# Attention and FFN, forward and backward on one core: filling products split into four 32-column tiles in half of the steps, and backward stores issued from SP

## The chip, the core and the metric

The kernel runs on one core of one Trainium2 chip. The metric is the device time of one execution in microseconds (us); three runs of the kernel before gave 1441.34 us as the median, from 1441.24 to 1441.88. Five engines work beside each other, each with an instruction queue of its own that is run in order: PE (TensorE: matrix products and, as PEld, weight loads), DVE (VectorE), ACT (ScalarE), POOL (GpSimd) and SP (SyncE, which here only issues DMAs). Products land in PSUM, a small memory of banks of 128 partitions by 2 KB, and DVE or ACT have to read them out.

## The reference

The output is a block with two branches, and the gradients of all its inputs:

```
xn  = layernorm(x)                                     # x: 2048 x 448
out = x + softmax(q k^T / sqrt(28)) v wo + (silu(xn wg) * (xn wu)) wd
        with q, k, v = xn wqkv                         # 16 heads of 28
outputs: out, and d(out)/d(x, wqkv, wo, wg, wu, wd) applied to grad_out
```

All inputs and outputs are bf16. The FFN is 448 x 1792. In the attention backward, per head, P = exp(q k^T / sqrt(28)) is computed again, dP = dO v^T, dS = P * (dP - delta), dV = P^T dO, dK = dS^T q, dQ = dS k; the division by the softmax sums is folded into dO.

## The kernel before

A forward part comes first, up to about 620 us. It computes attention and FFN, transposes, and spills what the backward part needs to DRAM. It is not touched by the change. The backward part runs from about 620 to 1397 us, and a tail of some 40 us finishes the gradient of x.

**The order of the backward part is written by hand, in one loop (L1231) over steps k.** The heads are taken in 4 groups g of 4 heads, in 2 pairs hp per group. Per pair there are 4 blocks of 512 keys (kc) by 16 blocks of 128 queries (qc, qi): 512 steps in all. Four steps (qi = 0 to 3) are called a block here, 128 in all. The text names a step by m = k % 4: step 1, 2, 3, 0. Each step issues, in this order:

- `row(k)` (L804): for two heads the scores sb (L812) of step k, and dP as db (L820) of step k-1. Each is a 32-row by 128-column tile of the array with 512 moving columns; the four lie beside each other in the array.
- `ew(k)` (L832): ACT takes the exponential of both sb into e_sb (L836); DVE multiplies both db of step k-1 with it into ds_sb (L842); SP issues a DMA transpose of ds_sb into dsT (L829), in three of four steps.
- `flush(k)` (L799): the stores that have been held for two steps. `drop()` (L757): SP issues some of the loads that are due later.
- `kv(k)` (L904, two in step 1 and two in step 2 for the most part): dV and dK, four products per call, each in a 128-row by 32-column tile of the array (L915, L919), accumulated in the bank acc.
- in step 1 `dq_unit` (L936): dQ from dsT, 16 products in 32-column tiles (L946), evacuated by ACT (L959 or L950), added up by POOL (L961, L963).
- in step 0 `tr_unit` (L892): eight PE transposes of the fourth ds_sb (L897), in full 128 x 128 form, copied by ACT (L902).

**Filling products.** Between these, PE gets products of other parts, here called F: `late_dw` (L881), `y_unit` (L1072, the output), `dx_unit` (L1128) and `dc_unit` (L1172) (two parts of the gradient of x) and `dwq_unit` (L1011, the gradient of wqkv). Each is a generator that issues one product per piece, with 128 x 128 weights and 256 to 448 moving columns. `fill_open` (L1209) takes the next unit, `fill_step(room)` (L1219) issues pieces until the room in ns is used up. Step 2 issues one or two pieces (R2 = 250), right behind the two `kv` calls; step 3 four to six (R3 = 750), behind the `row`; step 0 two or three (R0 = 400) ahead of the transposes and the rest of the unit behind them. So a block holds one unit. There is one bank genb for the units and dQ together. When a unit is done, DVE or ACT reads genb.

**Buffers that set the order.** Three banks for sb, freed by the exponential three products before; three for db and the transposes together, freed by DVE's L842 (or ACT's L902); ten buffers ds_sb, freed when `kv`, the transposes and the DMA transpose have read them; three buffers dsT.

**Stores.** `store(o, i)` (L795) puts a store on a list, and `flush` issues it two steps later from POOL (L802): dkv and dqT (to DRAM, for `dc_unit` later), y, the gradients of wqkv (dwq_o) and the last slice of the FFN weight gradients. There are 76 of them, up to 128 KB each. In the tail `store` issues at once.

Of the kernel before, what the change touches and what calls it, by code (L numbers as in the profile page):

```python
# [17 lines left out]
D = 448  # L18
# [3 lines left out]
G = 4  # L22
HP = 32
NT = S // 128
NFC = F // 128
P = 128
# [77 lines left out]
def kernel(  # L104
# [23 lines left out]
    PE, DVE, ACTE, POOL, SP = nc.tensor, nc.vector, nc.scalar, nc.gpsimd, nc.sync  # L128
# [19 lines left out]
    xn_sp = xn_t[:, :NT * D].rearrange("p (t d) -> p t d", d=D)  # L148
# [399 lines left out]
    for i in range(len(chain) + LEAD):  # L548
# [4 lines left out]
        k = i - LEAD  # L553
# [100 lines left out]
    for t in range(4):  # L654
        run(T_unit(xnT, xn_t, t, t % 2 == 0, ps_s if t < 2 else None))
    DVE.tensor_reduce(out=r_ones[:],
                      in_=ident_f[:].rearrange("p (a b) -> p a b", b=HP)[:, :, 28:30],
# [11 lines left out]
    for c in range(3):  # L669
        k = 4 * c  # L670
        t = 4 * c + 4
# [100 lines left out]
    def have(*keys):  # L772
        for x in [x for x in slow if x[1] in keys]:
            slow.remove(x)
            SP.dma_start(out=x[2], in_=x[3])
# [19 lines left out]
    def store(o, i):  # L795
        held.append((now + 2, o, i))
        flush(0 if now < NB else 10 ** 9)

    def flush(upto):  # L799
        while held and held[0][0] <= upto:  # L800
            _, o, i = held.pop(0)
            POOL.dma_start(out=o, in_=i)  # L802

    def row(k):  # L804

# [51 lines left out]
    k = n = 0  # L857
# [14 lines left out]
    fT = bk.tile([P, 4, 2, 4, P], BF16, name="dsp", bufs=1)  # L872
# [3 lines left out]
    def late_dw(c):  # L876
        d0, dn = DCH[c]
        have(("f",))
        ps = ps_g.tile([P, 2, P], FP32, name="genb")
        for t in range(NT):  # L880
            PE.matmul(ps[:dn], lhsT=xn_sp[:, t, d0:d0 + dn], rhs=fT[:, t // 4, :, t % 4, :],  # L881
                      start=(t == 0), stop=(t == NT - 1))
            if t < NT - 1:
                yield 110
        DVE.tensor_copy(out=w2[:dn, c], in_=ps[:dn])
        for a, o in enumerate((out_4, out_5)):
            store(o[d0:d0 + dn, F - P:], w2[:dn, c, a])
        yield 110

    dq_acc = bk.tile([P, S // 2], FP32, name="dq_acc", bufs=1)  # L890

    def tr_unit(b):  # L892
        for qi in (3,) if b < NB // 4 - 1 else (2, 3):
# [93 lines left out]
    dsp = {}  # L987
# [19 lines left out]
    def dwq_unit(g, c, tag="genb"):  # L1007
        d0, dn = DCH[c]
        ps = (ps_b if tag == "rest" else ps_g).tile([P, 3 * P], FP32, name=tag, bufs=2 if tag == "rest" else 1)
        for t in range(NT):  # L1010
            PE.matmul(ps[:dn, :], lhsT=xn_sp[:, t, d0:d0 + dn], rhs=dsp[g][:, t].rearrange("p k r -> p (k r)"),  # L1011
                      start=(t == 0), stop=(t == NT - 1))
            if t < NT - 1:
                yield 162
        o = bk.tile([P, 3, 4, DH], BF16, name="dwq_o")
        p4 = ps[:].rearrange("p (k h r) -> p k h r", k=3, r=HP)
        cp = ACTE.copy if tag == "rest" else DVE.tensor_copy
        cp(out=o[:dn, 0], in_=p4[:dn, 0, :, :DH])
        cp(out=o[:dn, 1:3, 0:2, :], in_=p4[:dn, 1, :, :DH].rearrange("p (k h) r -> p k h r", k=2))
        cp(out=o[:dn, 2, 2:4, :], in_=p4[:dn, 2, 0:2, :DH])  # L1020
        cp(out=o[:dn, 1, 2:4, :], in_=p4[:dn, 2, 2:4, :DH])
        store(wq_out[d0:d0 + dn, :, g * 4 * DH:(g + 1) * 4 * DH],
              o[:dn].rearrange("p k h r -> p k (h r)"))
        s_done.add((g, c))
        yield 162
# [4 lines left out]
    NH = NFC // 2  # L1030
    ych, yts = {}, {}
# [16 lines left out]
    wd_sb = yp.tile([P, NFC, D], BF16, name="wd_sb", bufs=1)  # L1048
    wo_sb = yp.tile([P, G, D], BF16, name="wo_sb", bufs=1)
# [10 lines left out]
    def y_unit(ch, half, ti):  # L1060
        if ti == 0:
            have(("y", ch, half))
            nxt = 2 * ch + half + 2
            if nxt < 8:
                load_y(nxt // 2, nxt % 2)
        tsl = slice(ti * P, (ti + 1) * P)
        mm = [(ych[ch, half][:, i, tsl], wd_sb[:, half * NH + i, :]) for i in range(NH)]
        if half:
            mm += [(ych[ch, 3][:, i, tsl], wo_sb[:, i, :]) for i in range(G)]
        ps = ps_g.tile([P, 512], FP32, name="genb")  # L1070
        for i, (l, r) in enumerate(mm):
            PE.matmul(ps[:, :D], lhsT=l, rhs=r, start=(i == 0), stop=(i == len(mm) - 1))  # L1072
            if i < len(mm) - 1:
                yield 189
        if half == 0:
            yts[ti] = yp.tile([P, D], FP32, name="yt", bufs=5)
            DVE.tensor_tensor(out=yts[ti][:], in0=ps[:, :D], in1=ych[ch, 2][:, ti, :], op=ALU.add)
        else:
            y = yp.tile([P, D], BF16, name="y")
            DVE.tensor_tensor(out=y[:], in0=ps[:, :D], in1=yts[ti][:], op=ALU.add)  # L1080
            store(out0_d[:, 4 * ch + ti, :], y[:])
        yield 189


    dxs = {}
# [22 lines left out]
    def load_dx(ch, fq):  # L1108
        f0, f1 = FQ[fq]
        if ch == 2 and fq < 2:  # L1110
            load_w(fq + 1, now + 32)
        d = dxs["pool"].tile([P, 5, 2, 512], BF16, name="dau_c")
        drip(("dx", ch, fq), [(d[:, i - f0:min(i + 2, f1) - f0], F_d[ch, :, i:min(i + 2, f1), 1:3, :]) for i in range(f0, f1, 2)], now + 16)
        dxs[ch, fq] = d

    def dx_unit(ch, fq, ti):
        if ti == 0:
            have(("dx", ch, fq))
            nxt = 4 * fq + ch + 1
            if nxt < 12:  # L1120
                load_dx(nxt % 4, nxt // 4)
        d = dxs[ch, fq]
        f0, f1 = FQ[fq]
        n = 2 * (f1 - f0)
        tsl = slice(ti * P, (ti + 1) * P)
        ps = ps_g.tile([P, 512], FP32, name="genb")
        for i in range(n):
            PE.matmul(ps[:, :D], lhsT=d[:, i // 2, i % 2, tsl], rhs=dxs["w", fq][:, i // 2, i % 2, :],  # L1128
                      start=(i == 0), stop=(i == n - 1))
            if i < n - 1:  # L1130
                yield 189
        o = dxs["g"][:, 4 * ch + ti, :]
        if fq == 0:
            ACTE.copy(out=o, in_=ps[:, :D])
        else:
            DVE.tensor_tensor(out=o, in0=ps[:, :D], in1=o, op=ALU.add)
        yield 189
# [3 lines left out]
    dcs, dy2 = {}, {}  # L1141
# [23 lines left out]
    def dc_unit(t):  # L1165
        if t % 4 == 0:
            have(("dc", t // 4))
            if t < 12:
                load_dc(t // 4 + 1)
        ps = ps_g.tile([P, 512], FP32, name="genb")  # L1170
        for i in range(3 * G - 3):
            PE.matmul(ps[:, :D], lhsT=dcs[t // 4][:, i, (t % 4) * P:(t % 4 + 1) * P], rhs=dxs["wq"][:, i, :],  # L1172
                      start=(i == 0), stop=(i == 3 * G - 4))
            if i < 3 * G - 4:
                yield 189
        DVE.tensor_tensor(out=dxs["g"][:, t, :], in0=ps[:, :D], in1=dxs["g"][:, t, :], op=ALU.add)
        yield 189
# [41 lines left out]
    def fill_step(room):  # L1219
        nonlocal cur  # L1220
        if cur is None:
            return
        for ns in cur:
            room -= ns
            if room < ns / 2:
                return
        cur = None
# [3 lines left out]
    for k in range(NB + 12):  # L1231
        now = k
        if k < NB:
            g, hp, kc, qc, qi = steps[k]
            if hp == 1 and kc > 0 and qc == 2 and qi == 2 and g + 1 < G:
                load_k(g + 1, kc - 1)
            if g > 0 and hp == 0 and kc == 0 and qc == 2 and qi == 2:
                load_k(g, 3)
            if hp == 1 and g + 1 < G and qi == 3 and (kc, qc) in NEXT:
                load_q(g + 1, NEXT.index((kc, qc)))  # L1240
        m = k % 4
        if k <= NB:
            if k >= K0:
                row(k)
                ew(k)
            flush(k)
            if 2 <= k:
                drop()
        if m:
            while kv_n < NB and kv_n <= k - (2 if m == 2 or kv_n % 16 == 15 else 3) and (m != 2 or kv_n % 16):  # L1250
                kv(kv_n)
                kv_n += 1
        if m == 0:
            b = (k - 8) // 4
            if 9 <= k < NB and cur is None:
                fill_open(600)
            fill_step(R0)
            if 0 <= b < NB // 4:
                tr_unit(b)
            fill_step(BIG)  # L1260
        elif m == 1:
            b = (k - 13) // 4
            if 0 <= b < NB // 4:
                dq_unit(b)
        elif m == 2:
            if 9 <= k < NB:
                fill_open(BIG)
                fill_step(R2)
        else:
            fill_step(R3)  # L1270
    while stream:
        for _ in stream.pop(0)[1]():
            pass
# [14 lines left out]
    g = G - 1  # L1288
# [96 lines left out]
```

## Time and profile before

| | |
|---|---|
| median of 3 runs | 1441.34 us |
| the profiled execution | 1441.88 us, of which the span from the first to the last instruction is 1440.1 us |
| mean granted TensorE clock | 0.985 |
| busy: PE / ACT / DVE / POOL | 92% / 88% / 80% / 28% of the span |
| busy from 1100 to 1200 us: PE / DVE / ACT | 96.8 / 95.3 / 94.1 us of 100 |
| busy from 690 to 890 us: PE / DVE / ACT | 187.6 / 183.4 / 182.1 us of 200; DMA engines 1.16 |
| time of a block in the backward part | 5.6 to 7 us, mostly 5.63 to 6.1 |

How it is read: a line of the profile's groups gives line, engine, operation, tiles out<-in, shapes and count, then busy us and the mean ns of one, then the engine's idle time just before these instructions with what ended it. "32*128" in front of a shape is the tile of the array that a product uses (rows * columns). A timeline line gives start and length in us; equal instructions that follow each other are merged, and a wait stands in brackets. A product's record lasts some 180 ns longer than its share of the array, since products are pipelined: what counts is the distance of starts. The DMA share is the mean busy share of 16 DMA engines; it passes 1 since packets of two queues, or neighbours of one queue, overlap.

### The profile page before, as it was taken

What the parts mean: (1) busy time and instruction counts of PE and PEld (TensorE: products, weight loads), DVE (VectorE), ACT (ScalarE), POOL (GpSimd) and SP (SyncE); (2) the same over time, 40 slices, a digit from 0 to 9 for tenths busy, and PEclk for the clock granted to TensorE, in tenths of its full rate; (3) what the DMA queues carried; (4) which work ended last, traced back from release to release, by engine and by line L of the source; (5) the groups of instructions that cost most, each with busy time, mean ns of one, the idle gap of its engine ahead of it and who ended that gap; (6) DMA issues with size and microseconds to landing.
All of it is one profiled execution on the core that took longest, in us unless ns stands there. A gap on an engine that the chain in (4) does not pass through costs nothing. (4 is left out here: it accounts for less than half of the span.)

```text
span 1440.1 us, 34682 instructions
## 1 busy us (share of the span) xinstructions
PE 1326.3 (92%) x12647; PEld 541.0 (38%) x12708; DVE 1151.8 (80%) x1997; ACT 1261.5 (88%) x2193; POOL 403.6 (28%) x561
## 2 busy tenths in 40 slices
PE   5889999999999999889999999999999999999996
PEld 2333333333333333333333434433443444444343
DVE  6667757666676676578998998888889999989988
ACT  5789988988889999869989989899989999989974
POOL 6464524464334454111112112201111011010006
PEclk9999999999999999989999999999999999999998
DMA  5796956796678586799999999999999999999971
GB/s 154 181 199 165 235 122 160 187 195 164 146 162 192 147 172 145 178 234 226 226 213 217 232 220 188 196 209 229 228 173 194 209 223 230 201 191 203 198 142 60
DMA packets 681179, 271.69 MB, mean 189 GB/s; under 512 B 606424, under 2 KB 655824, under 8 KB 681008
## 3 DMA queue, kind: packets, MB, share of 16 engines
q1 hardware_dynamic: 672576, 255.35, 87.1%
q0 software_dynamic: 7024, 13.82, 4.1%
q8 instruction: 100, 1.64, 0.5%
q14 instruction: 71, 0.58, 0.1%
q10 hardware_dynamic: 1408, 0.30, 0.1%
HBM read 65.09 MB, written 60.36 MB: 87 GB/s over the span
## 5 line engine op out<-in xcount | busy, mean ns | idle before, releaser
L842 DVE TENSOR_TENSOR ds_sb<-db,e_sb 128x512 bf16<-128x512 f32 x1024 | 646.8, 684 | 51.3 <-issue 21.1
L836 ACT ACTIVATE e_sb<-sb 128x512 bf16<-128x512 f32 x1024 | 554.8, 611 | 60.4 <-PE db L820 44.5
L612 ACT ACTIVATE eT<-s_w 128x1024 bf16<-128x1024 f32 x256 | 263.5, 1029 | 46.1 <-PE s_ps L609 43.1
L614 ACT ACTIVATE eT<-s_ps 128x512 bf16<-128x512 f32 x512 | 280.4, 612 | 0.0
L820 PE MATMUL db<-kd,qd 32*128 32x512 bf16 x1024 | 234.4, 384 | 8.2 <-DVE ds_sb L842 7.4
L812 PE MATMUL sb<-kd,qd 32*128 32x512 bf16 x1024 | 210.4, 387 | 5.1 <-DMA qd<-QD_d 3.3
L961 POOL TENSOR_TENSOR dq_acc<-dq_acc,dq_st 128x256 f32<-128x256 f32 x64 | 46.2, 721 | 455.4 <-ACT dq_st L959 455.4
L919 PE MATMUL acc<-ds_sb,qd 128*32 128x512 bf16 x1024 | 161.0, 391 | 0.0
L915 PE MATMUL acc<-e_sb,qd 128*32 128x512 bf16 x1024 | 158.8, 391 | 1.3 <-DVE dw_o L528 1.3
L902 ACT COPY dsT<-db 128x1024 bf16<-128x1024 bf16 x128 | 130.1, 1016 | 14.6 <-PE db L897 13.9
L380 POOL TENSOR_TENSOR nn<-nn,ag 128x512 f32<-128x512 f32 x56 | 71.2, 1271 | 252.2 <-DVE ag L378 243.7
L609 PE MATMUL s_ps<-QQ,KK 32*128 32x512 bf16 x512 | 125.4, 385 | 3.9
L1128 PE MATMUL genb<-wguT,dau_c 128*128 128x448 bf16 x448 | 117.5, 355 | 6.3 <-ACT dq_st L959 3.9
L609 PE MATMUL s_w<-QQ,KK 32*128 32x512 bf16 x512 | 100.3, 387 | 13.1 <-ACT eT L612 10.4
L812 PEld LDWEIGHTS <-qd 32*128 32x128 bf16 x1024 | 48.2, 91 | 149.4 <-issue 140.3
L421 PE MATMUL gen<-xn_t,f_sp 128*128 128x448 bf16 x416 | 91.8, 354 | 2.6 <-DVE nn L395 1.7
L421 PEld LDWEIGHTS <-f_sp 128*128 128x128 bf16 x640 | 55.7, 98 | 75.0 <-issue 31.9
L946 PE MATMUL genb<-dsT,kd 128*32 128x256 bf16 x2048 | 79.5, 275 | 1.9 <-DVE dqT L955 0.6
L897 PE MATMUL db<-ident_bf,ds_sb 128*128 128x128 bf16 x1032 | 79.4, 220 | 1.1 <-DVE ds_sb L842 1.1
L897 PEld LDWEIGHTS <-ds_sb 128*128 128x128 bf16 x1032 | 68.3, 99 | 24.1 <-issue 5.3
L451 PE MATMUL gen<-eT,VS 128*32 128x512 bf16 x1024 | 68.4, 384 | 5.5 <-DVE nn L395 3.3
L381 POOL TENSOR_TENSOR nn<-nn,tt 128x512 f32<-128x512 f32 x56 | 72.0, 1286 | 4.4
(167 smaller groups left out, 1911.0 us busy)
## 6 DMA issues: line engine op xcount, KB each, us to landing
F_d<-hda SPq DMA_DIRECT2D x56, 384.0 KB, 3.1
dau_c<-F_d SPq DMA_DIRECT2D x24, 512.0 KB, 4.4
qd<-QD_d SPq DMA_DIRECT2D x16, 512.0 KB
kd<-KD_d SPq DMA_DIRECT2D x16, 384.0 KB, 4.0
dsT<-ds_sb SPq DMA_TRANSPOSE x383, 4.3
dc<-dqkvT_d SPq DMA_DIRECT2D x12, 384.0 KB, 3.9
h_c<-F_d SPq DMA_DIRECT2D x8, 512.0 KB, 4.4
wT_d<-wT_f SPq DMA_DIRECT2D x14, 256.0 KB, 3.6
```

The costliest lines, as they stand in the source:

```text
L421: PE.matmul(ps[:, :D], lhsT=fsp[fc][:, t // 4, w, t % 4, :], rhs=rhs[:, t, :], start=(t == 0), stop=(t == NT - 1))
L609: PE.matmul(sp4[hh], lhsT=KK[g][r:r + HP, kt * P:(kt + 1) * P], rhs=QQ[g][r:r + HP, qsl], start=True, stop=True, tile_position=(r, 0))
L612: ACTE.activation(out=e2[0][:], in_=wide[:], func=ACT.Exp, scale=SCALE)
L614: ACTE.activation(out=e2[1][:, j], in_=sp4[2 + j], func=ACT.Exp, scale=SCALE)
L812: PE.matmul(s_ps[:], lhsT=qside[g, qc][r:r + HP, 0, qi * P:(qi + 1) * P], rhs=kside[g, kc][r:r + HP, 0, :], start=True, stop=True, tile_po ...
L820: PE.matmul(d_ps[:], lhsT=qside[g, qc][r:r + HP, 1, qi * P:(qi + 1) * P], rhs=kside[g, kc][r:r + HP, 1, :], start=True, stop=True, tile_po ...
L836: ACTE.activation(out=est[k][:, j], in_=sps.pop((k, j))[:], func=ACT.Exp, scale=SCALE)
L842: DVE.tensor_tensor(out=ds[:, j], in0=dps.pop((k - 1, j))[:], in1=est[k - 1][:, j], op=ALU.mult)
L897: PE.transpose(ps[:, c, :], ds[:, c // 4, (c % 4) * P:(c % 4 + 1) * P], ident_bf[:])
L902: ACTE.copy(out=o, in_=ps[:])
L915: PE.matmul(a[r:r + HP, :], lhsT=sp4[:, 1, r:r + HP], rhs=e[:, j, :], start=first, stop=last, tile_position=(0, r), skip_group_check=True)
L919: PE.matmul(a[r:r + HP, :], lhsT=sp4[:, 0, r:r + HP], rhs=ds[:, j, :], start=first, stop=last, tile_position=(0, r), skip_group_check=True)
```

## The change

Two things are changed.

1. Filling products go through a helper `mm`. In steps 2 and 3 (`split = m > 1`) it issues, in place of one product with 128 x 128 weights, four products with 128 x 32 weights, into the four 32-column tiles of the array and the matching 32 partitions of the same bank, with the same moving operand (two, where the weights have 64 columns). In step 0 it issues one full product as before. The transposes that are used as fillers (dsp, dsq) stay full.
2. `flush` issues stores from SP in place of POOL.

```diff
     def flush(upto):
         while held and held[0][0] <= upto:
             _, o, i = held.pop(0)
-            POOL.dma_start(out=o, in_=i)
+            SP.dma_start(out=o, in_=i)
...
+    split = False
+
+    def mm(ps, lhsT, rhs, start, stop):
+        if not split:
+            PE.matmul(ps, lhsT=lhsT, rhs=rhs, start=start, stop=stop, skip_group_check=True)
+            return
+        for c in range(0, lhsT.shape[1], HP):
+            PE.matmul(ps[c:c + HP], lhsT=lhsT[:, c:c + HP], rhs=rhs, start=start, stop=stop,
+                      tile_position=(0, c), skip_group_check=True)
...
         for i in range(n):
-            PE.matmul(ps[:, :D], lhsT=d[:, i // 2, i % 2, tsl], rhs=dxs["w", fq][:, i // 2, i % 2, :],
-                      start=(i == 0), stop=(i == n - 1))
+            mm(ps[:, :D], d[:, i // 2, i % 2, tsl], dxs["w", fq][:, i // 2, i % 2, :], i == 0, i == n - 1)
             if i < n - 1:
                 yield 189
...
         m = k % 4
+        split = m > 1
```

The same replacement of `PE.matmul` by `mm` is made in `late_dw`, `dwq_unit`, `y_unit` and `dc_unit`. After the loop `split` is set to False again, so that the tail uses full products. Budgets and the order of the pieces stay: the list of instructions of the built program has 12,702 products before and 14,442 after. Each of the 112 units now begins in 32-column tiles directly behind the 32-column tiles of `kv`; 600 full products became sets of four (30 of them sets of two).

## The prediction

> **What bounds the kernel now.** First the busy times: PE leads over the whole span.
>
> ```profile
> PE 1326.3 (92%) x12647; PEld 541.0 (38%) x12708; DVE 1151.8 (80%) x1997; ACT 1261.5 (88%) x2193; POOL 403.6 (28%) x561
> ...
> L842 DVE TENSOR_TENSOR ds_sb<-db,e_sb 128x512 bf16<-128x512 f32 x1024 | 646.8, 684 | 51.3 <-issue 21.1
> L836 ACT ACTIVATE e_sb<-sb 128x512 bf16<-128x512 f32 x1024 | 554.8, 611 | 60.4 <-PE db L820 44.5
> ```
>
> But the change lies in the backward part alone, and there PE, DVE and ACT are nearly level (96.8, 95.3 and 94.1 of 100 us from 1100 on). So I read one block from the timelines of PE and DVE:
>
> ```profile
> 1100.46 0.39 PE L812 MATMUL sb<-kd,qd 32*128 32x512 bf16 x2
> 1100.47 0.39 PE L820 MATMUL db<-kd,qd 32*128 32x512 bf16 x2
> ...
> 1101.02 0.38 PE L919 MATMUL acc<-ds_sb,qd 128*32 128x512 bf16 x2
> 1101.34 0.36 PE L1128 MATMUL genb<-wguT,dau_c 128*128 128x448 bf16 x1
> 1101.63 0.39 PE L812 MATMUL sb<-kd,qd 32*128 32x512 bf16 x2
> 1101.64 0.49 PE L820 MATMUL db<-kd,qd 32*128 32x512 bf16 x2
> 1102.06 0.93 PE L1128 MATMUL genb<-wguT,dau_c 128*128 128x448 bf16 x4
> 1102.92 0.39 PE L812 MATMUL sb<-kd,qd 32*128 32x512 bf16 x2
> ...
> 1104.38 0.80 PE L820 MATMUL db<-kd,qd 32*128 32x512 bf16 x2
> ```
>
> ```profile
> 1101.01 3.75 DVE L842 TENSOR_TENSOR ds_sb<-db,e_sb 128x512 bf16<-128x512 f32 x6 [0.16 <-issue]
> 1104.68 0.62 DVE L1136 TENSOR_TENSOR dxg<-genb,dxg 128x448 f32<-128x448 f32 x1
> 1105.21 1.28 DVE L842 TENSOR_TENSOR ds_sb<-db,e_sb 128x512 bf16<-128x512 f32 x2
> ```
>
> Two things are to be seen. **PE pays about 0.1 us whenever the tile shape changes.** The last dV/dK set starts at 1101.02, the filling product F at 1101.34: 0.32 us, though 512 columns last 0.213 (dQ's 16 products show the rate: four sets of 256 columns, start to start 109 ns each). Over the backward part the excess has a median of 99 ns from dV/dK to F (112 times), 98 from F to the row products (320) and -6 from dV/dK to dQ, where the shape stays (126). **And DVE is the stricter engine.** From 1101.01 to 1106.49 it has no gap: six products for steps 2, 3 and 0, one evacuation, two products for step 1. PE waits for it: the second db product of step 1 starts at 1104.79, not beside its pair at 1104.38, because its bank is freed by DVE's last product of step 0. DVE's one gap, 0.16 us, stands in front of step 2, at the end of PE's longest stretch (that db product, four dV/dK sets, dQ, the next row); no F lies in it. The circuit is six DVE products (3.79 us) plus this stretch with its two hand-overs (1104.70 to 1106.64, 1.94 us): 5.73 against blocks of 5.63 to 6.1.
>
> Sorted by step, over the last 117 blocks, DVE's waits in front of L842 are 21.2 us for step 2, 9.3 for step 1, 8.1 for step 0 (31 waits over 50 ns) and 4.3 for step 3 (29 waits).
>
> **The change, part by part.**
>
> *The switch behind dV/dK (A).* It goes in all 112 units: 112 x 0.098 = 11.0 us of PE. What the end gets of it: the row of step 3 comes 0.1 us earlier, and DVE uses that only where it waits for step 3; wait by wait the smaller of the wait and 98 ns sums to **2.6 us**. It goes no further down PE: in the block above the second db product of step 3 starts 0.10 us behind its pair, since it needs the bank that DVE's first product of step 2 frees, and in 101 of 111 blocks a second product of that row is held so by DVE or ACT. Those will wait longer by what the row gains, and the four F and the row of step 0 start when they did. I take -2.6; the ends are 0 and -11.0.
>
> *Leaving the tiles (B).* Four tiles start some 10 ns apart, and after dV/dK the change to the row takes 107 ns from the last start, against 98 after F. In steps 2 and 3 that is 224 x 9 ns = 2.0 us of PE, felt where DVE waits for the rows that follow (59 of 222): +0.5; ends 0 and +2.0.
>
> *The sets themselves (C).* 600 products become sets of four. PE's distance of F is 189 ns for 448 columns; no row has four tiles of 448. dQ's sets take 109 ns for 256 columns, 2 more than the columns; the first dV/dK set to the second takes 226 for 512, 13 more than the columns. So 0 to 600 x 11 = +6.6 us of PE; below nothing it cannot be, as 448 columns last 187 ns. I take 0, as for dQ, where several sets follow each other as they will in step 3. Eight instructions per set fit: dQ's go through in 109 ns.
> The Trainium skill speaks against it: "TensorE: Matmul & The Clock Gate", section "Wait — 56ns, not 53.3ns?", gives about 62 ns of the sequencer for each product when hardware decoding is off. Four would then take 248 ns, and my estimate from that page is 600 x 59 ns = 35 us more PE work. The 27 ns per product of dQ's row decide against it here.
>
> *The wait that moves.* A unit's first product waits, as before, for ACT to free genb from dQ (in the built program it stands on the first tile alone). In the block ACT is done at 1101.03 and F would start at 1101.24: cover of 0.2 us. Where it is gone, A's gain in that block goes, nothing more.
>
> *Stores from SP (D).* 76 stores leave POOL (16.8 us of POOL for the 29 between 690 and 890 us). POOL is 28% busy and its sums are not waited for; 0 there. On SP each takes what a load takes, 0.57 us (L769), or 0.33 like the last stores (L1338). SP's list puts them behind the transposes of the same step, with data two steps old, so they do not wait for data; behind them are the next transposes and loads. Who waits for those: DVE for ds_sb buffers, dQ for dsT. From 690 to 890 us there is no room on SP: 102 transposes take 169.9 us and 27 loads 17.4, 187.3 of 200, and transposes are issued 4 to 10 us after their data is ready. DVE already waits there ten times, 5.2 us, when neither PE nor ACT is late; the list of waits puts 3.4 us of it down to the DMA of dsT, which has still to read the buffer. 29 stores x 0.57 = 16.5 us would not fit, but for this: 43.4 of the 169.9 us lie above the 1.24 us that an unhindered transpose takes. That is SP held up by full DMA engines, and a store's issue can lie in it.
>
> ```profile
> q1 hardware_dynamic: 672576, 255.35, 87.1%
> q0 software_dynamic: 7024, 13.82, 4.1%
> ```
>
> In the same 200 us q1 (SP's) has a share of 108.5% and q0 (POOL's) 6.4%; the stores pass from the second to the first. For the engines the work stays: a y store is 32 packets of 146 or 350 ns on q0, 0.50 us on each of 16 engines; as 128 packets of 54 ns (896 B on q1) it is 0.43; a dkv store is 0.44 against 0.49. So I take +1.0 for D; the ends are 0 and +16.5.
> The skill's "DMA: Bandwidth & Descriptors", section "Issuing engines are not separate DMA queues", says that issuing from several engines saves only the issue time; by it D would be exactly the question of SP's time, and 0 if the held-up time takes it in.
>
> *Tail.* Four POOL issues (2.8 us) go; POOL's next sum waits for ACT after each, so 0.
>
> **Sum:** -2.6 + 0.5 + 0 + 1.0 = -1.1 us. The profiled execution took 1441.88 us (span 1440.1, 1.8 around it), 0.5 above the median; taken from the median of 1441.34 that is **1440.2**.
>
> **Rivals.**
> - *PE is the bound after all (faster).* For it: PE is the busiest, and ACT waits 30.3 us in front of step 0's exponentials, in 108 of 117 blocks, for a row behind four F. Against it: that row is tied to DVE through step 3. If half of the 11.0 us arrived: 1435.8; all of it: 1430.3.
> - *SP becomes the bound (slower).* Place: 690 to 890 us, 0.85 stores a block. It decides from the point where the transposes' held-up time does not shrink by what the stores add: then SP falls 0.85 x 0.57 = 0.48 us further behind per block, uses up the 1 to 2 us that dsT still has before dQ within four blocks, and every later block is longer by it. Half of 16.5 with A's gain: 1441.3 - 2.1 + 8.3 = 1447.5; all of it 1455.7. For it: the lag, and these ten waits. Against it: the 43.4 us.
> - *The split does nothing.* If the 98 ns stay although the shape no longer changes, A is 0: 1442.8. Against it: dV/dK to dQ, -6.
>
> **Numbers.** A measurement of this kernel can tell about 0.2% (2.9 us) from no change. My forecast, a change within that (1438.5 to 1444.2, the third rival in it): 0.47. PE as the bound: 0.28. SP as the bound: 0.25, with C at its upper end counted in. The range for 8 in 10 reaches to half of the first rival and half of the second: 1434.5 to 1448.
>
> **What would show it.** A is right if the starts from the last dV/dK set to the first F lie 213 ns apart, not 320, and if the second db product of step 3 waits 0.1 us longer; wrong if the row of step 0 moves up with it. C: starts of sets of four 189 ns apart. D: the transposes' lengths from 690 to 890 us shrink by some 16 us, the lag stays below 10 us, and DVE's waits for buffers stay near 5 us; if these grow to 10 or more, the second rival holds. A clock under 1.0 in the backward part, or waits of F for ACT, would make all of it wrong.

## The result, and the profile after

The changed kernel takes **1455.06 us** (median of 4 runs, 1452.97 to 1460.46) against 1441.29 (4 runs, 1439.69 to 1441.88): 1.0103 of the time before, with a 95% interval of 1.0074 to 1.0132. It is 14 us slower; the forecast was 1440.2 us with a range up to 1448. The time lies at the full price of the rival "SP becomes the bound" (1455.7). The profiled execution took 1452.97 us with a span of 1451.2, 11.1 longer than before.

From the page of the changed kernel, the lines that answer to those of before:

```profile
PE 1329.5 (92%) x14387; PEld 555.7 (38%) x14448; DVE 1152.0 (79%) x1997; ACT 1259.4 (87%) x2193; POOL 361.6 (25%) x485
...
q1 hardware_dynamic: 691328, 263.34, 90.0%
q0 software_dynamic: 3568, 5.83, 1.8%
...
L842 DVE TENSOR_TENSOR ds_sb<-db,e_sb 128x512 bf16<-128x512 f32 x1024 | 646.9, 684 | 51.7 <-issue 21.2
L836 ACT ACTIVATE e_sb<-sb 128x512 bf16<-128x512 f32 x1024 | 553.1, 614 | 62.0 <-PE db L820 52.0
```

DVE, ACT and POOL have no more to do, PE is busy 3.2 us longer, and DVE's idle time before L842 is the same to 0.4 us. (SP only issues, so it has no row of this kind.) Sums over the span hide the loss. One block of a calm stage, from PE's and then DVE's timeline of the changed kernel:

```profile
1111.17 0.38 PE L928 MATMUL acc<-ds_sb,qd 128*32 128x512 bf16 x2
1111.38 0.36 PE L898 MATMUL genb<-wguT,dau_c 128*32 128x448 bf16 x4
...
1112.21 0.94 PE L898 MATMUL genb<-wguT,dau_c 128*32 128x448 bf16 x16
1113.08 0.39 PE L812 MATMUL sb<-kd,qd 32*128 32x512 bf16 x2
...
1114.54 0.81 PE L820 MATMUL db<-kd,qd 32*128 32x512 bf16 x2
```

```profile
1111.16 3.75 DVE L842 TENSOR_TENSOR ds_sb<-db,e_sb 128x512 bf16<-128x512 f32 x6 [0.16 <-issue]
1114.83 0.61 DVE L1143 TENSOR_TENSOR dxg<-genb,dxg 128x448 f32<-128x448 f32 x1
1115.37 1.28 DVE L842 TENSOR_TENSOR ds_sb<-db,e_sb 128x512 bf16<-128x512 f32 x2
```

The last dV/dK set and the first filling set start 0.21 us apart, not 0.32: the change of shape is gone, and four sets (16 products) take the time of four full ones. DVE's block is the one of before, down to the gap of 0.16 us. So here PE got faster, and DVE did not.

The loss is elsewhere. Blocks 2 to 24 (650 to 783 us before) are 12.6 us longer, and the rest of the backward part is 2.6 shorter. Around 720 us DVE stops for 3.79 us (DVE's timeline, then SP's queue, then PE's timeline, of the changed kernel):

```profile
715.55 3.90 DVE L842 TENSOR_TENSOR ds_sb<-db,e_sb 128x512 bf16<-128x512 f32 x6
723.25 0.62 DVE L1088 TENSOR_TENSOR y<-genb,yt 128x448 bf16<-128x448 f32 x1 [3.79 <-DMA out_dram<-y]
```

```profile
715.71 3.12 SPq L829 DMA_TRANSPOSE dsT<-ds_sb  x2
718.87 0.58 SPq L802 DMA_DIRECT2D out_dram<-y  x1
719.89 1.59 SPq L829 DMA_TRANSPOSE dsT<-ds_sb  x1
```

```profile
723.93 0.91 PE L955 MATMUL genb<-dsT,kd 128*32 128x256 bf16 x16 [3.08 <-DVE y L1088]
```

The tile y has two buffers. Its first three sums come in consecutive blocks, and the third must wait until the first store has read its buffer. That store now stands in SP's list behind transposes that are issued some 6 us after their data are ready: the first sum was made at 707.96, its store leaves at 718.87, and DVE goes on 4.4 us after that. (In the kernel before POOL issued this store 2.5 us after its sum.) DVE waits, genb stays full, dQ behind it waits, and PE stands for 3.08 us. The list of DVE's waits of the changed kernel from 640 to 1396 us shows for which DMAs DVE waited (us in total, times, longest):

```profile
DVE y L1088 <- DMA out_dram<-y: 8.2, 3, 3.8
DVE ds_sb L842 <- DMA dsT<-ds_sb: 6.9, 7, 2.2
DVE dwq_o L1026 <- DMA out_dram<-dwq_o: 1.9, 2, 1.1
```

In the kernel before there is one such line:

```profile
DVE ds_sb L842 <- DMA dsT<-ds_sb: 3.4, 4, 1.0
```

**And each stop costs a second time.** The table by windows of the changed kernel (window, its length, busy us of PE, PEld, DVE, ACT, POOL, then the granted clock, the DMA share and GB/s):

```profile
710.00:720.00 10.00, 10.00 (x132) 4.07 (x124) 9.04 (x15) 9.37 (x17) 1.27 (x2) 1.00 1.30 213
720.00:730.00 10.00, 6.69 (x69) 3.38 (x66) 6.22 (x10) 5.36 (x11) 0.72 (x1) 0.71 0.97 204
730.00:740.00 10.00, 10.00 (x148) 4.52 (x150) 9.01 (x15) 9.18 (x18) 1.46 (x2) 0.95 1.13 224
```

Behind the stop the clock is halved from 724.1 to 731.0 us: 5.9 of the 10 us in the second window at half the clock give 0.71. The records of the clock come in stretches of 3.41 us. From block 2 on, the changed kernel has nine such stretches at half the clock, the kernel before three.

### What a halved stretch costs, and what brings it

A stretch at half the clock also comes without a wait for a DMA. In the kernel before, at a change of the pair of heads (windows of 3.4 us, columns as above):

```profile
914.90:918.30 3.40, 2.34 (x25) 1.14 (x24) 3.35 (x6) 3.22 (x7) 1.82 (x3) 1.00 1.14 203
918.30:921.70 3.40, 3.40 (x41) 2.05 (x40) 2.83 (x5) 2.00 (x3) 0.00 (x0) 0.50 1.44 139
921.70:925.10 3.40, 3.40 (x35) 1.04 (x28) 2.66 (x6) 2.74 (x6) 0.72 (x1) 1.00 0.65 121
```

For each stretch I added up the products (columns by the share of the array that their tile takes) in 18 traces, all but those of p1_loads_pool and p2_swap below, from 650 to 1405 us. The sum is given as a share of what full 128 x 128 products could fill. In 62 cases the clock fell to one half in the next stretch. Every stretch filled to less than 0.35 was followed by half the clock, none above 0.39 was. (In the two traces left out all 26 falls lie below 0.37; one stretch there that was itself at half the clock, filled to 0.30, was followed by the full clock.) In calm places the blocks around a halved stretch last 1.04 to 1.27 us longer than the same blocks in the other traces (11 cases, median 1.15).

With this price, an estimate where the place is not calm, the 11.1 us of span add up: six more halved stretches at 1.15 are 6.9; blocks 2 to 24 lose 6.8 besides, where DVE's listed waits for DMAs between 640 and 800 us are 13.7 us against 2.8 before; the forward part is 1.1 longer (its program is the same; in the other traces with the loads as before it lies between -1.7 and +5.5); and blocks 24 to the end gain 3.8.

One more thing follows for all that is below: single runs scatter with the clock. Among the runs of the kernel before that were made beside the experiments (123 runs, 1433 to 1451 us) each 0.001 of mean clock goes with 0.8 to 1.1 us. So the ratios below come from 6 to 12 runs each; only those of p1_loads_pool and p2_swap come from 2 and 5 of their 6 runs, because runs over 1.5% above the fastest of the same kernel count as slow ones and are left out. The mean clock of the kernel before is 0.983 to 0.984, that of the changed kernel's four runs 0.979, and that of e1 to e6 and s1 0.980 to 0.981; part of their loss goes with it. For most of the others it is given below.

### The profile page after: what moved, and what is told of

Same layout as the page of the kernel before. It is cut to its first block, busy times and chain, and to the rows that moved or that the text cites. A ratio compares the mean times of both kernels' runs of the same rounds, so it can differ in the third digit from the quotient of the medians.

```text
span 1451.2 us, 38114 instructions
## 1 busy us (share of the span) xinstructions
PE 1329.5 (92%) x14387; PEld 555.7 (38%) x14448; DVE 1152.0 (79%) x1997; ACT 1259.4 (87%) x2193; POOL 361.6 (25%) x485
## 5 line engine op out<-in xcount | busy, mean ns | idle before, releaser
L842 DVE TENSOR_TENSOR ds_sb<-db,e_sb 128x512 bf16<-128x512 f32 x1024 | 646.9, 684 | 51.7 <-issue 21.2
L820 PE MATMUL db<-kd,qd 32*128 32x512 bf16 x1024 | 239.9, 386 | 10.4 <-DVE ds_sb L842 9.6
L609 PEld LDWEIGHTS <-KK 32*128 32x128 bf16 x1024 | 28.9, 91 | 115.4 <-issue 111.8
```

The source lines that it names most:

```text
L609: PE.matmul(sp4[hh], lhsT=KK[g][r:r + HP, kt * P:(kt + 1) * P], rhs=QQ[g][r:r + HP, qsl], start=True, stop=True, tile_position=(r, 0))
L820: PE.matmul(d_ps[:], lhsT=qside[g, qc][r:r + HP, 1, qi * P:(qi + 1) * P], rhs=kside[g, kc][r:r + HP, 1, :], start=True, stop=True, tile_po ...
L842: DVE.tensor_tensor(out=ds[:, j], in0=dps.pop((k - 1, j))[:], in1=est[k - 1][:, j], op=ALU.mult)
```

## Experiments

All ratios are to runs of the kernel before on the same chip, with a 95% interval.

### One part alone

**e1_split_only**: the changed kernel, stores back on POOL.

```diff
-            SP.dma_start(out=o, in_=i)
+            POOL.dma_start(out=o, in_=i)
```

> The changed kernel with its stores on POOL again: the split alone. Theory 1 (the whole loss comes from the stores on SP; the split gives what the last 100 blocks of the changed kernel show, 13.6 us behind at block 24 and 9.7 at block 124): 2.5 to 4 us faster than before, ratio 0.997 to 0.998. Rival 2 (the split itself costs: its 1,740 more products and weight loads disturb PE): 3 us or more slower than before, ratio 1.002 and up.

Measured 1.0013 (0.9998 to 1.0028). No gain from the split.

**e2_stores_only**: the kernel before with its stores issued from SP (the other part of the change).

```diff
-            POOL.dma_start(out=o, in_=i)
+            SP.dma_start(out=o, in_=i)
```

> The kernel before with its stores on SP: the stores alone. Theory 1: 14 to 18 us slower than before, ratio 1.010 to 1.012, with waits of y's sum for the store of y around 720 and 780 us. Rival 2: within 3 us of before.

Measured 1.0047 (1.0031 to 1.0062); DVE waits 5.2 us for y and 4.1 for ds_sb. So moving the stores costs time by itself, 6.8 us, though less than half of what theory 1 expected. The two parts do not add up to the 1.0103 of both.

**e3_y_four_bufs**: the changed kernel, with four buffers for y.

```diff
-            y = yp.tile([P, D], BF16, name="y")
+            y = yp.tile([P, D], BF16, name="y", bufs=4)
```

> The changed kernel with four buffers for y in place of two. Theory 1a (most of the loss is DVE's sum of y waiting until the store of two units earlier has landed; in the changed kernel 7.4 us in two waits, and what PE loses behind them): 7 to 9 us faster than the changed kernel, about 1446, 4 to 6 us still lost in blocks 4 to 9. Rival 1b (SP itself is the bound, y's buffer is only where it shows): the waits pass to DVE's ds_sb and to dQ, at most 3 us gained.

Measured 1.0056 (1.0038 to 1.0074). The waits for y are gone, and the waits for ds_sb have grown (list of DVE's waits, 640 to 1396 us):

```profile
DVE ds_sb L842 <- DMA dsT<-ds_sb: 8.6, 8, 2.1
DVE dwq_o L1026 <- DMA out_dram<-dwq_o: 1.9, 1, 1.9
```

By the ratios (1.0103 for the changed kernel, from 4 runs) the two more buffers win 6.8 us, close to theory 1a; but 1.0056 stays with no wait for y left. So y's two buffers are at most a part of the loss, not the whole cause.

**e5_stores_act**: the changed kernel, with the stores issued from ACT.

```diff
-            SP.dma_start(out=o, in_=i)
+            ACTE.dma_start(out=o, in_=i)
```

> The changed kernel with the stores issued from ACT. Theory 1 (what costs is the place behind SP's list of transposes and loads): no waits for stores, so the split's gain is left, less what 76 issues cost ACT: 1437 to 1441. Rival 3 (what costs is the stores' packets, 128 short ones in place of 32 long ones, on the DMA engines whatever queue issues them): as slow as the changed kernel, 1452 to 1458.

Measured 1.0057 (1.0037 to 1.0078). SP is relieved (transposes are issued 2.6 us after their data, not 6.5), and DVE waits for no DMA. But here a store whose data are not ready stops ACT, which in the kernel before is busy for 46.2 of the 50 us from 640 to 690 (ACT's timeline):

```profile
656.79 0.98 ACTq L802 DMA_DIRECT2D out_dram<-dqT  x2
657.88 2.06 ACT L836 ACTIVATE e_sb<-sb 128x512 bf16<-128x512 f32 x4 [4.83 <-issue]
```

### Which stores

**e4_y_on_pool** and **e6_y_on_sp**: the changed kernel with y's 16 stores on POOL and the other 60 on SP, and the reverse.

```diff
-    def store(o, i):
-        held.append((now + 2, o, i))
+    def store(o, i, eng=SP):
+        held.append((now + 2, o, i, eng))
...
-            store(out0_d[:, 4 * ch + ti, :], y[:])
+            store(out0_d[:, 4 * ch + ti, :], y[:], POOL)
```

```diff
-    def store(o, i):
-        held.append((now + 2, o, i))
+    def store(o, i, eng=POOL):
+        held.append((now + 2, o, i, eng))
...
-            store(out0_d[:, 4 * ch + ti, :], y[:])
+            store(out0_d[:, 4 * ch + ti, :], y[:], SP)
```

> The changed kernel, but the 16 stores of y leave from POOL; the other 60 stay on SP. In the changed kernel DVE waits 8.2 us, in three places, for the store of an older y that stands behind transposes on SP, and the array's clock is halved behind two of these waits. Theory 1 (y's two buffers): no wait of DVE for y is left, the blocks that lasted 7.2 and 10.7 us last 5.6 to 6.5, and the kernel stands like the one with the split alone: 1.001 to 1.003 of the time before. Theory 2 (each store on SP sets the transposes back, whichever it is; with four y buffers the wait only moved to ds_sb): the waits for ds_sb stay at 6 to 9 us, 1.005 or more.

> The counterpart: only the 16 stores of y leave from SP, the other 60 from POOL, with the split. Theory 1 (y's two buffers): DVE waits again some 5 to 8 us for y in two or three places, and nearly all of the loss is there: 1.006 to 1.010. Theory 2 (SP's load): 13 of the 29 stores between 690 and 890 us, so less than half of the loss, 1.002 to 1.004.

Measured 1.0083 (1.0061 to 1.0105) without y's stores on SP and 1.0061 (1.0045 to 1.0076) with them alone. In the first DVE waits 9.2 us for ds_sb and never for y; in the second 6.0 for y and 1.3 for ds_sb. Theory 1 falls: each group of stores on SP costs. How much of the loss goes with y's buffers stays open: e3, with all stores on SP, has a smaller ratio than e4, and their intervals overlap.

### SP's time or the bytes

**s1_tiny**: the kernel before, with a DMA of 128 bytes from SP beside each store.

```diff
             POOL.dma_start(out=o, in_=i)
+            SP.dma_start(out=scr.pop(0), in_=ident_bf[0:1, 0:64])
```

> The kernel before, whole filling products and all stores from POOL, with one DMA of 128 bytes issued from SP beside each of the 76 stores (it writes 64 constants to an unused place in DRAM). SP gets the instructions of the stores without their bytes and without their buffers. Theory 2a (SP's time and order: each further issue sets the transposes back, and DVE waits for ds_sb): the waits for ds_sb rise from 3.4 to 6 us or more and the time is 1.003 to 1.005, as with the stores moved and no split (1.0047). Theory 2b (the stores' bytes in SP's ring, between the transposes' packets): 1.000 to 1.001.

Measured **1.0072** (1.0047 to 1.0097), as much as moving the stores. The waits for ds_sb are 12.0 us. The longest stands behind this (SP's queue, then DVE's timeline):

```profile
734.90 7.09 SPq L832 DMA_TRANSPOSE dsT<-ds_sb  x3
742.04 0.57 SPq L769 DMA_DIRECT2D o_c<-OT_d  x1
742.72 3.15 SPq L832 DMA_TRANSPOSE dsT<-ds_sb  x2
745.92 0.43 SPq L805 DMA_DIRECT2D scr_d<-ident_bf  x1
```

```profile
741.84 2.48 DVE L845 TENSOR_TENSOR ds_sb<-db,e_sb 128x512 bf16<-128x512 f32 x4 [2.65 <-DMA dsT<-ds_sb]
```

So neither bytes nor buffers of the stores are needed for the loss: 76 more DMAs in SP's list are enough. Whether it is SP's time or the place that they take in the order of its DMAs, this run does not separate. SP's queue from 690 to 890 us, added up from the traces:

| kernel | transposes: number, us, mean | loads, us | stores: number, us | all, us |
|---|---|---|---|---|
| before | 102, 169.8, 1.67 | 17.4 | - | 187.3 |
| changed | 95, 151.9, 1.60 | 16.8 | 25, 17.2 | 185.8 |
| e2 | 98, 154.8, 1.58 | 16.2 | 25, 15.1 | 186.1 |
| s1 | 96, 159.8, 1.66 | 16.1 | 25, 11.2 | 187.1 |
| e5 | 99, 160.5, 1.62 | 20.3 | - | 180.7 |

But for e5 the last column hardly moves: SP is full, with 186 to 187 us of 200 (the 13 us that are left are 0.1 us for each of 130 issues), and what is added pushes transposes out of the window. 95 in place of 102 is 2.3 blocks of 5.9 us, 13.8 us. The count alone would only say that the blocks are longer; that SP's list makes them so is shown by s1. Of the 17.2 us of stores the transposes took in 6.2 (95 x 0.065); of the tiny ones' 11.2 they took in less than 1.

**p1_loads_pool** and **p2_swap**: the spread loads moved from SP to POOL, in the kernel before and in the changed one.

```diff
             _, _, o, i = slow.pop(0)
-            SP.dma_start(out=o, in_=i)
+            POOL.dma_start(out=o, in_=i)
```

> The kernel before, with the loads that are spread over the steps issued from POOL in place of SP: the opposite of the change, SP is left with the transposes. Theory 2a or 2b (SP's queue or ring is what ends last in the stage from 690 to 890 us): the waits for ds_sb (3.4 us before) go, and the time is 0.996 to 0.999. If the DMA engines themselves are what is full there, whichever queue feeds them, the waits stay: 1.000, or more where a load on POOL lands later.

> The changed kernel, with the same spread loads moved from SP to POOL: stores and loads change places, so that SP has no more instructions than before. Theory 2 (SP's load): the waits for ds_sb fall to 3 us or less; what is left are y's waits, 5 to 8 us with the halved clock behind them: 1.003 to 1.006. Theory 3 (a store in SP's ring hurts by itself, since transposes behind it must wait for it): no better than the changed kernel, 1.008 to 1.012.

Measured 1.0315 (1.0277 to 1.0353) and 1.0399 (1.0365 to 1.0432). All theories were wrong here. With large loads in POOL's queue the transposes themselves get longer: 1.97 us on the average in p2_swap between 690 and 890 us, against 1.60 in the changed kernel, and in places this (SP's queue of p2_swap):

```profile
742.45 14.38 SPq L829 DMA_TRANSPOSE dsT<-ds_sb  x5
```

Five transposes took 14.38 us, 2.9 each. A likely reason, not tested by itself, is that their packets then share the DMA engines with a second queue of long packets. So in this kernel loads of 384 to 512 KB are better off in SP's own list; moving them is no way to make room there.

**f4_one_load**: the kernel before, with the two loads of each half of h_c in one.

```diff
-                               for a, b in ((0, 4), (4, 7))], due)
+                               for a, b in ((0, 7),)], due)
```

> The kernel before with each half of the FFN activations for y (7 x 128 KB) loaded by one DMA in place of two: the same bytes in SP's ring, eight issues less in the stage from 640 to 870 us. Theory 2a (SP's time and order): 8 x 0.57 = 4.6 us less on SP, the waits for ds_sb (3.4 us) shrink, 0.998 to 0.999. If eight issues are too few, or a load of 896 KB holds the transposes up by itself: 1.000 to 1.002.

Measured 1.0028 (1.0004 to 1.0051) at a mean clock of 0.9807 against 0.9833. Six loads fewer in the window (21 for 27), and the transposes grow to 1.72 us each: no room is won this way either. So SP's list costs time when it grows; no run here wins time by making it shorter.

### Where the split's gain is

**e8_split_step2** and **e9_split_step3**: the split in one of the two steps, stores on POOL.

```diff
-        split = m > 1
+        split = m == 2
```

```diff
-        split = m > 1
+        split = m == 3
```

> Split in step 2 alone (one or two products right behind the dV/dK products), full products in step 3, all stores on POOL: the part of the change that takes the change of shape away, without the sets of step 3. The record's step A says -2.6 us and B 0.2: 0.998 to 0.999, with PE's 99 ns from dV/dK to the filling product gone. The rival is that the row of step 3 comes earlier and something else takes the place: then 1.000. A second rival: the split kernel lost what it gained to the array's clock (mean 0.980 over 12 runs against 0.984 over 25 of the kernel before, and 0.82 us of time for each 0.001 of clock among the latter, so 2.8 us); if the sets of step 3 are what lowers the clock, here the clock is 0.983 to 0.984 and the time 0.998; if the step that is nearer to its limit lowers it, 0.980 and 1.000 to 1.001.

> Split in step 3 alone (four to six products behind the row), full products in step 2, all stores on POOL: no change of shape is taken away, since the products behind dV/dK stay full; what is left are the sets. By the record's steps B and C: 0 to +0.4 us, 1.000, with sets 189 ns apart. If the sets lower the array's clock: 0.980 and 1.002.

Measured 1.0010 (0.9996 to 1.0025) and 1.0029 (1.0012 to 1.0046), at clocks of 0.9825 and 0.9833 (before 0.9840). The -2.4 us of steps A and B are outside the first interval. The sets of step 3 cost more than the 0 to 0.4 us that were expected, though PE needs hardly more for them: set to set 192 ns on the average, full product to full product 193, and 10 ns more in front of each row, 1.1 us in all.

**w1_warm**: a test of the clock. The kernel before, with products that nobody reads, in PE's waits at the changes of pairs and at the end.

```diff
+    def warm(k, n):
+        s_ps = pre[k, 0] = ps_b.tile([P, 512], FP32, name="sb", bufs=3)
+        g, hp, kc, qc, qi = steps[min(k, NB) - 1]
+        for _ in range(n):
+            PE.matmul(s_ps[:], lhsT=ident_bf[:], rhs=kside[g, kc][:, 0, :], start=True, stop=True)
...
+            if k % 64 == 4 and 64 < k < NB:
+                warm(k + 1, 3)
...
+            if k % 64 == 2 and 64 < k < NB:
+                warm(k + 1, 4)
```

> The kernel before, with 52 products that nobody reads, in places where PE waits anyway: four and three at each of the seven changes of the pair of heads (steps 64j+2 and 64j+4), three at the end of the loop. They write a bank of sb that the next row overwrites. In ten profiles every stretch of 3.41 us in which the products (columns by tile area) filled less than 0.36 of the array was followed by half the clock for the next 3.41 us, and those with over 0.385 never were; each such stretch in a calm place made the blocks around it 1.04 to 1.27 us longer. Theory clock: the products keep the array over the limit there; of about 1.3 such stretches per run at the changes of pairs and 0.7 at the end (1.4 us), most go: mean clock up by 0.001 to 0.002 and 0.998 to 0.999 of the time. If the halved clock is only a sign of waiting and costs nothing itself: same clock, 1.000 or, by the 52 x 0.21 us of products, up to 1.003.

Measured 0.9996 (0.9981 to 1.0011). The mean clock rose from 0.9826 to 0.9854 (standard errors 0.0006 and 0.0004), and in its trace one halved stretch is left after block 2. So more products keep the clock up, as the filling rule says. That the time follows the clock is likely from the scatter of single runs (-2.5 us by it), but here it is -1.0 +- 1.0 us on the means, so not shown.

**f1_step2_warm** and **f2_split_warm**: e8 and e1 with the same products (the first line of the diff is f1's alone).

```diff
-        split = m > 1
+        split = m == 2
...
+            if k % 64 == 2 and 64 < k < NB:
+                warm(k + 1, 4)
```

> Split in step 2 alone, all stores from POOL, and the 52 unread products at the changes of pairs and at the end, which raised the mean clock from 0.9826 to 0.9854 without the split. Theory 4 (the split's gain is there and was eaten by the array's clock): with the clock at 0.985 or more the 2.4 us of step A come out: 0.998. Theory 5 (the gain is not there, since what ends last in these steps is tied to DVE and ACT): 1.000, whatever the clock, within the 0.0004 that the unread products gave by themselves.

> The split of the change (steps 2 and 3), all stores from POOL, and the same 52 unread products. Theory 4: 0.998 at a clock of 0.985. Theory 5: 1.000 to 1.001; if the sets of step 3 have a price of their own (0.0029 when they alone were split), 1.002.

Measured 0.9979 (0.9957 to 1.0001) at a clock of 0.9854, and 1.0023 (1.0000 to 1.0045) at 0.9823; before 0.9833. The medians of the first are 1440.55 and 1440.24 us, so no gain can be read off it yet; the second speaks against theory 4.

**f3_more_pe**: the kernel before with 107 ns more of PE at the start of each unit, behind dV/dK. (The edit is made in the changed kernel's `mm`, with `split` False throughout and the stores on POOL.)

```diff
+        if start and now < NB:
+            wide = len(rhs.shape) > 2
+            PE.matmul(ps if wide else ps[:, :256], lhsT=lhsT, rhs=rhs if wide else rhs[:, :256],
+                      start=True, stop=True, skip_group_check=True)
```

> The kernel before with one product more at the start of each of the 112 units: 256 columns with the unit's first weights into genb, which the unit's first product overwrites, so 0.107 us of PE behind dV/dK in each block, 12.0 us in all, the mirror of step A. Theory 5 (PE's time at this place does not reach the end): 1.000 to 1.002. If PE's time at this place counts in full, and A failed for another reason: 1.008; by half 1.004.

Measured 1.0055 (1.0033 to 1.0077), at a mean clock of 0.9817: more than half of the 12.0 us. PE's time at this place is thus not free. And it depends on the stage. With 1.15 us taken off per halved stretch, blocks 41 to 124 are 4.1 us longer than before, and blocks 2 to 41, which scatter by some 5 us between traces, 3.7 us shorter. There the transposes are issued 4.0 us after their data (median; 6.5 before), and no wait of DVE for a transposed ds_sb is left. So a slower PE seems to let SP keep up.

That pointed to a split by place. **g1_split_late** and **g2_split_early**: f2 with the split from step 181 on, and up to step 180.

```diff
-        split = m > 1
+        split = m > 1 and k > 180
```

```diff
-        split = m > 1
+        split = m > 1 and k <= 180
```

> All stores from POOL, the 52 unread products, and the split of the change from step 181 on (block 42 and later), where SP has room between the transposes. In the traces so far, with 1.15 us taken off for each stretch at half the clock, blocks 41 to 66 and 100 to 124 last 154.5 to 154.7 and 143.0 to 143.4 us without the split and 153.7 to 154.0 and 142.1 to 142.5 with it. Theory 6 (the split gains what step A said where DVE waits for PE, and loses it where the transposes bound the blocks): 0.998, with those two sums as in the split kernels. Theory 5 (nothing reaches the end): 0.9996, as with the unread products alone.

> The counterpart: the split up to step 180 alone, in the stage in which SP is full. Theory 6: the rows of step 3 come 0.1 us earlier, DVE and SP are no faster, so 1.000 if the gain is only lost there, and 1.001 to 1.003 if a faster PE makes waits of another kind there (more waits for ds_sb than 3 us, a lower clock). Theory 5: 1.000.

Measured **0.9974 (0.9959 to 0.9989)** late and **1.0025 (1.0009 to 1.0041)** early, at the same mean clock (0.9848 and 0.9846; before 0.9833). Theory 6 holds: both carry the same unread products, and the place of the split alone makes 6.0 us between them (on the means, standard error 1.0). g1 beats both kernels: 1438.50 us (12 runs) against 1441.17 for the kernel before. Some of it may belong to the unread products. The stages of the traces, in us, with 1.15 off per halved stretch:

| kernel | blocks 24-41 | 41-66 | 66-100 | 100-124 |
|---|---|---|---|---|
| before | 103.8 | 154.7 | 202.8 | 143.1 |
| e2, no split | 101.6 | 154.5 | 202.7 | 143.0 |
| w1, no split | 102.6 | 154.7 | 203.0 | 143.4 |
| g2, split early | 103.7 | 154.6 | 203.0 | 143.4 |
| e1, split | 101.1 | 153.8 | 203.6 | 142.1 |
| f2, split | 103.1 | 154.0 | 202.9 | 142.5 |
| g1, split late | 104.0 | 154.1 | 202.6 | 142.5 |
| changed | 102.9 | 153.7 | 201.6 | 142.2 |

In these traces blocks 41 to 66 and 100 to 124 are shorter where the split is on in them, by 0.4 to 1.3 us each. Of the traces with the split that are not in the table, e4's is an exception, with 155.2 in the first of them, and e6's (154.4) hardly differs. Over blocks 41 to 124 six traces without the split there have a mean of 500.8 us, eight with the whole split 499.5. In blocks 24 to 41 the traces scatter by 3 us and show nothing.

## Why the prediction was wrong

**D (stores on SP, +1.0, ends 0 and +16.5): this is the step that failed.** The rival had the right bound and place, and named what would decide: whether "43.4 of the 169.9 us" by which the transposes are held up would take the stores in. They took in 6.2 of 17.2. Alone, D measured 6.8 us (e2, 4.5 to 8.9), with the split some 13 (the changed kernel against e1), where +1.0 was taken. The held-up time belongs to each transpose, not to a pool of spare time: with 95 instead of 102 it went from 0.43 to 0.36 us each. s1_tiny, whose 11.2 us were not covered at all and which costs as much, shows that more issues in SP's list are price enough. I had the addition in hand (187.3 + 16.5 of 200) and let an average argue it away. The sign that was set for D was no good either: the transposes' lengths shrank by 17.9 us, as they were to ("some 16"), but 11.7 of it is that seven fewer fitted in.

Two terms were missing in it. Behind a store there are also **the store's own buffers**: "who waits for those: DVE for ds_sb buffers, dQ for dsT" leaves out y, whose two buffers now hang on a list that lags by 6 us. They are the place of 8.2 us of waits; e3 takes these away and the ratio falls from 1.0103 to 1.0056, while e4, with y off SP, stays at 1.0083. So they may have a share in the price; these runs do not settle its size. And **the clock**: the prediction says that a clock under 1.0 in the backward part would make all of it wrong. It was under 1.0 in nine stretches, and six more than before cost some 6.9 of the 11.1 us in the profiled execution. The rival's picture, blocks that get longer by 0.48 us each, is not what happened either. The lag stays at 6.6 us in the median (6.5 before) and below 10, as foretold, and the loss comes in stops of 1 to 4 us with a halved clock behind them. The clock was in neither rival's price, so that the time meets 1455.7 is partly chance. The sign that counted was "10 or more" of waits for buffers: 17.0 us in the list, 3.4 before.

**A and B (-2.6 and +0.5): right in size where DVE waits for PE, absent elsewhere.** Over the whole kernel the split alone measured +1.9 us (e1, -0.3 to +4.0), not -2.1. The 98 ns are gone where a unit starts behind dV/dK (excess -7 ns), and sets start as close as full products (C is 0). Leaving the tiles costs 98 ns from the last start, as after dQ in the kernel before; but the last of four tiles starts 10 ns after the first, so a set holds PE 10 ns longer than a full product does. Over 219 such places that is 2.2 us, B's size, though not for its reason ("107 ns from the last start"). In front of step 3 ACT waits 3.0 us in place of 8.1, and in front of step 0 37.2 in place of 30.3: the gain is handed on and stands before the next row, as the step said. In blocks 41 to 124 some 1.4 us come out (standard error 0.5), about the share (83 of 117 blocks) of the 2.1 that A and B make (1.5). What the step did not see is the stage: in blocks 2 to 41 a faster PE meets an SP that is already full. g2 measures +3.2 us there (on the means +3.0). How it comes to more than nothing is not settled; in its trace the longest wait for ds_sb is 3.2 us, against 1.0 before, but other traces without the split have such waits too.

**The moved wait and the tail**: next to nothing, as predicted. The filling products' listed waits for ACT are 12.5 us, 11.7 before, and from the last dQ product to the end it is 41.9 us in both. The "circuit" of 5.73 us counted 0.1 us twice: by DVE's lines 3.75 us and the 1.88 to the next six products make 5.63, the length of that block. No term rests on it.

**PE as the bound** (-5.5 or -11 us) is out: the best kernel with the split wins 2.7 us, the unread products included. The reverse does not follow: PE time added at the same place counts by more than half (f3).

**The pages of the Trainium skill.** By the 62 ns for a product that "TensorE: Matmul & The Clock Gate", section "Wait — 56ns, not 53.3ns?", gives for hardware decoding off, the sets would have been an estimated 59 ns dearer each; 192 against 193 ns show none of it here. "DMA: Bandwidth & Descriptors", section "Issuing engines are not separate DMA queues", says that another issuing engine saves only the issue time. Here more issues on a full engine were price enough (s1), which agrees; but which engine issues also decided for which list a source buffer waits, and loads in POOL's queue went with slower transposes on SP (p2). The first page's section "What's actually happening" gives free-running windows of 3413 ns and half the clock after an idle one. The traces agree on the length and the half. They differ in that the window need not be idle: 0.29 to 0.38 of the array was enough in most of the 62 cases, with PE busy 2.34 of 3.40 us in the example above.

**Open**: why the split early costs 3 us; why the stores cost 4.7 per mille (thousandths of the time) without the split and 9 with it (changed kernel against e1; the intervals touch); how much of it is y's buffers; whether the unread products alone win time.

## What to carry to other kernels

Before moving DMAs to another engine, add up that engine's queue in the tightest stage: where issues already filled 187 of 200 us, more of them cost time, even with 128 bytes each (76 cost 7 per mille), and the first to stop was a tile of two buffers behind the list. A gain on one engine should be applied by stage: the same split, with the same unread products, made the kernel 2.7 us faster in the later blocks, where PE was waited for, and 3.2 slower in the earlier ones, where SP was full. And a stop of 3 us on PE is to be priced at 3 us and the halved clock behind it, some 1.2 us for each stretch of 3.4 by the estimate above.

## What the hardware showed beside this

- The array's clock fell to one half for 3.41 us whenever the products had filled less than 0.35 of the array in the 3.41 us ahead, and never above 0.39 (62 cases in 18 traces). A narrow tile counts by its share, so PE can be busy 70% of the time and still lose its clock: of the 3859 stretches that kept the full clock, 28 lie below the highest filling that was followed by half of it, but 222 when the time in which any product streams is counted in place of the filling.
- A DMA of 128 bytes holds SP for 0.43 us (s1), a store of 112 to 128 KB for 0.53 to 0.62 (medians by kind, changed kernel).
- Issues of DMA transposes went from 1.60 to 1.97 us on the average when large loads ran in POOL's queue in place of SP's (changed kernel and p2_swap, 690 to 890 us).
- Four products of 32 columns of weights that lie beside each other start in 189 ns, as one full product of 448 columns does.
